# Seven block products summed in PSUM for six pairs of chunks, and the first batch's scores with tokens on partitions

## Chip, core and metric

One core of a Trainium2 chip runs the whole kernel in one launch. The metric is the device time of one execution in microseconds; the median of several runs is compared. TensorE is PE in the profile, VectorE DVE, ScalarE ACT, GpSimd POOL; SyncE (SP) issues the DMAs.

## What is computed

Three stages follow each other: an attention over 32 learned memory slots, a two-layer product with a leaky activation, and a bilinear product. Four batches of 8 heads, 576 tokens and 64 dimensions give 2304 tokens of 512 values.

```python
a = exp(phi - max(phi, axis=2)); a = a / (sum(a, axis=2) + 1e-9)      # over the tokens
k_m = einsum('bhsm,bhsd->bhmd', a, k); v_m = einsum('bhsm,bhsd->bhmd', a, v)
scores = q @ k_m.T / sqrt(64)                                          # 32 per token and head
attn = softmax(scores); x = attn @ v_m                                 # then to (2304, 512)
h = x @ w_in; g = maximum(0.01 * h, h); x = g @ w_out                  # 512 -> 2048 -> 512
out = ((x @ w_a) * (x @ w_b)) @ w_out2                                 # 512 -> 1536 -> 512
```

All values are float32, except that the five weights arrive as 64-bit words, whose two halves the kernel joins into float32 itself.

## The kernel before

Values lie with features on partitions and tokens along the free dimension, so that every product's output is the next one's moving operand. A float32 operand is split in a high and a low part of type fp32r (a copy, on ACT or DVE, and a subtraction), and a product runs as three passes (PASSES, L771): high by high, high by low, low by high. Only in the first chunk for the first batch (FULL, `whole`, L722) are the products plain float32 matmuls, which need no split.

**Attention.** `kv_part` (L547) loads phi, keys and values of a batch and a half of its heads (g), takes the exponential, turns it on PE (ta, tz), sums keys and values against it (km, L603), normalises (kvn), turns again (kvt) and puts the results in kd (for the scores) and vm (for the values), with two copies each. `sc_both` (L653) does the scores of a piece of tokens (320 or 256 columns): the matmuls of L667 leave memory slots on partitions and tokens along the free dimension, so DVE turns them in blocks of 32 (L688), takes the maximum over 32 (L697), subtracts it (L698), ACT takes the exponential (L699), DVE sums (L702 to L704), multiplies (L707) and turns back into the tile at (L711). `vw_unit` (L732) multiplies vm by w_in, so that the attention's last product and the first layer are one: h is made from at and vw (`h_unit`, L803 for the first batch, L821 for the rest).

**The first layer pair.** Four chunks of 512 of the 2048 hidden values (c = 0 to 3), eight pieces of tokens each, in the order 0, 1, 2, ...; for each piece four h units and then four y units (`y_unit`, L867 and L871), one for each 128 rows of the 512 outputs (e). Each y unit reads all four tiles wout of its chunk. `weight` (L451) loads a tile of 128 rows (512 KB) and joins the words with two ACT and four DVE operations.

**The bilinear product.** The 2304 tokens are cut into two sets s of four blocks (2 x 2 of 512 tokens each) and a remainder of 256. For each set there are 12 chunks of 128 of the 1536 hidden values. `ab_unit` (L1076) makes both factors with seven products of a Strassen-Winograd scheme in place of eight, each six matmuls of 512 columns (L1092), in three PSUM banks X, Y and Z; the bank X is a running sum out of which ACT copies after three of its four products (L1103). The remainder goes the plain way (`left_unit`). The last product, by w_out2, works on pairs of chunks. In the plain way `o_unit` (L1168) does eight units of six matmuls (L1186) and DVE adds each into an accumulator in SBUF (L1199). For the pairs of the first eight chunks of the second set (`by_seven`, SEVEN = 8) it goes by seven block products: `w2_sums` makes four sums of the weights, `p_sums` four differences of the tokens and seven splits, and `o_part` (L1286) does product i for half x with three matmuls (L1301) in a PSUM bank of its own, which is added into one of seven accumulators osum (L1326); after the last pair, sums between the accumulators (L1318) make the four outputs. The stores are issued as soon as an output is complete (L1205); the last outputs are those of block l = 1, stored in two parts of 320 and 192 columns.

**The order of the work.** Nothing is ordered by hand. Each operation is given a cost, its tiles and its inputs, and a planner (`Program`, L108) simulates the five engines and lays out each engine's instructions before the kernel is built: the operation with the earliest due time that is ready goes next, on the engine among its candidates that would finish first. Due times come from a target order of the main products (`pos`), costs and handoffs, and are shifted by constants (SLACK for a load's or an operation's kind; START, LEAD, LAT, SPARE for the whole). Tiles get places (slots) as they come free, so a different order also moves loads. PE begins with WARM turns of the identity (L426), and `idle` puts groups of four turns (L434) in the start, each behind an operation whose result it reads: four groups on the tiles of w_in, four on the exponentials en, four on vwf.

Of the kernel before, what the change touches and what calls it, by code (L numbers as in the profile page):

```python
# [19 lines left out]
P = 128  # L20
# [5 lines left out]
EPS = 1e-9  # L26
# [28 lines left out]
TURN = 0.15  # L55
FILL = 4
WARM = 38
SEVEN = 8
LEAD = 37
SLACK = {'phi0': 72.94, ('kv0', 0): -15.48, ('kv0', 1): -17.72, 'kvr0': -10.62, ('q0', 0): 4.66, ('q0', 1): 32.32, ('win0', 0): 0.75, ('win0', 1): 103.86, ('wout0', 0): 20.54, ('wout0', 1): -39.84, 'win': -23.08, 'wout': 22.71, 'wa': -4.25, 'wb': -26.57, 'wout2': -2.14, ('sc', 0, 0): 57.16, ('sc', 0, 1): -2.31, ('sc', 1, 0): 13.24, ('sc', 1, 1): 6.37, ('sc', 2, 0): 23.27, ('sc', 2, 1): 24.61, ('vw', 0, 0): 85.06, ('vw', 0, 1): -56.75, ('vw', 0, 2): 18.69, ('vw', 1, 0): 5.23, ('vw', 1, 1): 100.39, ('vw', 1, 2): 9.67}  # L60
START = 15.05
BIAS = 0.52
POOL_BIAS = 9.26
LAT, LAT_SAME, LAT_DMA = 0.503, 0.134, 3.8
OVER = {'DMA': 0.0, 'PE': 0.0, 'ACT': 0.1, 'DVE': 0.019, 'POOL': 0.0}
BLOCKED = 2.31
DMA_RATE = 355000.0
SPARE = {'DMA': 1.27, 'PE': 1.0, 'ACT': 1.03, 'DVE': 1.03, 'POOL': 0.96}
# [39 lines left out]
class Program:  # L108
# [13 lines left out]
    def op(self, eng, cost, fn, r=(), w=(), tiles=(), pos=None, ahead=60.0, keep=0, slack=0.0, soon=False):  # L122
# [6 lines left out]
        o.slack, o.soon = slack, soon  # L129
# [206 lines left out]
def tile_mem_attention__leaky_mlp__bilinear_mlp(  # L336
# [93 lines left out]
    def idle(tile, get, token):  # L430
# [14 lines left out]
        "wout": lambda c, k: w_out[c * FC + k * P:c * FC + (k + 1) * P, :],  # L445
# [5 lines left out]
    def weight(kind, c, k, after=()):  # L451
# [73 lines left out]
    def phi_stats(b, gs, phi, st):  # L525
# [6 lines left out]
            r=e, w=nmx, tiles=[phi],  # L532
# [14 lines left out]
    def kv_part(b, g):  # L547
# [20 lines left out]
        if g == 0:  # L568
            tile_of(rest, "slot", [2, 512], parts=64)
            op("DMA", c_dma(64 * 4096), lambda T: nc.sync.dma_start(T[rest], kv_rest[b]), w=[rest], tiles=[rest], keep=6 if b else 0, slack=0 if b else SLACK["kvr0"])  # L570

# [20 lines left out]
        if b < 2:  # L592
            idle(en, lambda t: t[:, 0, :], (en, 0))
# [4 lines left out]
        def k_m(T):  # L598
            for t in range(5):
                n = P if t < 4 else 64  # L600
                src = T[kvt[t // 2]][:, t % 2, :] if t < 4 else T[rest][:, g, :]
                for h in range(4):
                    nc.tensor.matmul(  # L603
                        T[km][h * M:(h + 1) * M, :], T[en][0:n, t, h * M:(h + 1) * M], src[:, h * P:(h + 1) * P],
                        start=(t == 0), stop=(t == 4),
                    )

        op("PE", 1.5, k_m, r=[(en, 0), (en, 1), *kvt, rest], w=[km], tiles=[en, *kvt, rest, km])
# [21 lines left out]
        def ev_k(T, e):  # L630
# [526 lines left out]
    def by_seven(s, c):  # L1157
        return s == 1 and c < SEVEN

# [286 lines left out]
```

## Time and profile before

| | us |
|---|---|
| median of 3 runs | 787.47 (786.38 to 788.04) |
| the profiled execution's own time | 786.36 |
| its span, first to last instruction | 784.6 |

The profile is of one execution. The span is shorter than that execution's time by what lies around it. Rows below have times in us from the span's start, unless they say ns. In a timeline row the first number is the start, the second the time that the row's instructions take, and in brackets stands how long the engine was idle before and what released it. PEld are weight loads, which run beside the matmuls. The time of one matmul includes its passage through the array, which overlaps the next one's.

### The profile page before, as it was taken

What the parts mean: (1) busy time and instruction counts of PE and PEld (TensorE: products, weight loads), DVE (VectorE), ACT (ScalarE), POOL (GpSimd) and SP (SyncE); (2) the same over time, 40 slices, a digit from 0 to 9 for tenths busy, and PEclk for the clock granted to TensorE, in tenths of its full rate; (3) what the DMA queues carried; (4) which work ended last, traced back from release to release, by engine and by line L of the source; (5) the groups of instructions that cost most, each with busy time, mean ns of one, the idle gap of its engine ahead of it and who ended that gap; (6) DMA issues with size and microseconds to landing.
All of it is one profiled execution on the core that took longest, in us unless ns stands there. A gap on an engine that the chain in (4) does not pass through costs nothing.

```text
span 784.6 us, 12658 instructions
## 1 busy us (share of the span) xinstructions
PE 773.4 (99%) x4822; PEld 663.4 (85%) x4822; DVE 607.2 (77%) x1149; ACT 379.1 (48%) x817; POOL 0.7 (0%) x6
## 2 busy tenths in 40 slices
PE   7899999999999999999999999999999999999997
PEld 6567898989898988998888888888888888888886
DVE  5888988868888865686745899998995667898865
ACT  5767777747465635453445454445332254223210
POOL 0000000000000000000000000000000000000000
PEclk9999999999999999999999999999999999999999
DMA  9993331573247300035867547475488586978503
GB/s 321 384 323 140 99 90 61 192 264 103 82 174 266 124 1 1 1 115 206 293 247 267 185 160 273 161 239 190 164 322 346 178 275 209 354 250 280 179 19 108
DMA packets 56557, 149.99 MB, mean 191 GB/s; under 512 B 7216, under 2 KB 22576, under 8 KB 56496
## 3 DMA queue, kind: packets, MB, share of 16 engines
q1 hardware_dynamic: 56496, 149.18, 54.5%
q8 instruction: 38, 0.62, 0.3%
q14 instruction: 23, 0.19, 0.1%
HBM read 103.55 MB, written 45.61 MB: 190 GB/s over the span
## 4 chain that ended last, share of the span: by engine, by line
PE 95%; DMA 2%; DVE 1%; SPq 0%; ACT 0%; issue 0%
PE y L871 24%; PE abx L1092 17%; PE o L1186 13%; PE h L821 13%; PE abz L1092 8%; PE os L1301 5%; PE aby L1092 4%; PE b L1146 2%; PE a L1146 2%; PE y L867 2%; PE vw L750 2%; DMA kv<-in_kv_dram 1%; DMA phi<-in_phiT_dram 1%; PE h L803 1%; PE km L603 1%; PE sc L667 0%
## 5 line engine op out<-in xcount | busy, mean ns | idle before, releaser
L871 PE MATMUL y<-g,wout 128*128 128x320 f32 (+2 forms) x1104 | 197.2, 333 | 0.0
L871 PEld LDWEIGHTS y<-g,wout 128*128 128x128 f32 x1104 | 175.6, 188 | 16.7 <-issue 2.1
L1092 PE MATMUL abx<-yb_T,wo 128*128 128x512 f32 x432 | 109.7, 389 | 0.0
L1103 ACT COPY t<-abx 128x512 f32<-128x512 f32 x72 | 42.3, 587 | 122.7 <-PE abx L1092 117.6
L1092 PEld LDWEIGHTS abx<-yb_T,wo 128*128 128x128 f32 x432 | 80.6, 188 | 16.4
L1186 PE MATMUL o<-p,wout 128*128 128x512 f32 x384 | 93.6, 389 | 0.0
L1186 PEld LDWEIGHTS o<-p,wout 128*128 128x128 f32 x384 | 71.9, 188 | 15.2 <-DVE osum L1199 0.4
L774 ACT ACTIVATE g<-h 128x256 fp32r<-128x256 f32 (+1 forms) x120 | 49.7, 414 | 52.9 <-PE h L821 50.8
L821 PE MATMUL h<-ahi,vwh 128*128 128x256 f32 (+1 forms) x240 | 72.7, 303 | 0.0
L821 PE MATMUL h<-ahi,vwl 128*128 128x256 f32 (+1 forms) x240 | 71.0, 296 | 0.0
L821 PE MATMUL h<-alo,vwh 128*128 128x256 f32 (+1 forms) x240 | 71.0, 296 | 0.0
L890 DVE TENSOR_TENSOR acc<-y,acc 128x320 f32<-128x320 f32 (+1 forms) x72 | 40.1, 557 | 36.6 <-PE y L871 35.7
L837 DVE TENSOR_TENSOR g<-t,g 128x256 fp32r<-128x256 f32 (+1 forms) x120 | 53.7, 453 | 15.4 <-ACT t L774 14.4
L821 PEld LDWEIGHTS h<-ahi,vwh 128*128 128x128 f32 x240 | 45.4, 189 | 10.2 <-issue 3.6
L774 ACT ACTIVATE t<-h 128x256 f32<-128x256 f32 (+1 forms) x120 | 49.5, 413 | 0.0
L821 PEld LDWEIGHTS h<-alo,vwh 128*128 128x128 f32 x240 | 45.4, 189 | 0.2
L821 PEld LDWEIGHTS h<-ahi,vwl 128*128 128x128 f32 x240 | 45.5, 190 | 0.0
L1100 DVE TENSOR_TENSOR t<-abz,t 128x512 f32<-128x512 f32 x48 | 33.0, 688 | 13.2 <-PE abz L1092 7.6
L1199 DVE TENSOR_TENSOR oacc<-o,oacc 128x512 f32<-128x512 f32 x40 | 27.6, 690 | 16.7 <-PE o L1186 16.2
L1092 PE MATMUL abx<-yb_B,wo 128*128 128x512 f32 x144 | 36.9, 391 | 0.0
L1092 PE MATMUL aby<-yb_B,wo 128*128 128x512 f32 x144 | 36.7, 390 | 0.0
L407 ACT CAST p<-t 128x512 fp32r<-128x512 f32 x32 | 19.9, 621 | 34.7 <-DVE t L1124 22.7
(289 smaller groups left out, 1276.1 us busy)
## 6 DMA issues: line engine op xcount, KB each, us to landing
k_wo<-wo SPq DMA_DIRECT2D x32, 512.0 KB, 4.4
wo<-k_wo SPq DMA_DIRECT2D x32, 512.0 KB, 4.9
raw_wout<-in_w_out_dram SPq DMA_DIRECT2D x24, 512.0 KB, 5.5
raw_win<-in_w_in_dram SPq DMA_DIRECT2D x16, 512.0 KB, 5.2
kv<-in_kv_dram SPq DMA_DIRECT2D x16, 512.0 KB, 10.4
k_yb_T<-yb_T SPq DMA_DIRECT2D x8, 512.0 KB, 5.9
raw_wa<-in_w_a_dram SPq DMA_DIRECT2D x8, 512.0 KB, 4.5
raw_wb<-in_w_b_dram SPq DMA_DIRECT2D x8, 512.0 KB, 5.4
```

The lines of the kernel that those rows point to most:

```text
L774: nc.scalar.activation(dst, src, AF.Prelu, alpha=0.01)
L821: nc.tensor.matmul(T[o], T[w[u]][:, k, fs], T[a[v]][:, k, cols], start=(k == 0 and i == 0), stop=(k == 1 and i == 2))
L837: lambda T, e: engines[e].tensor_tensor(T[g][:, i, 1, to], T[t], T[g][:, i, 0, to].bitcast(F32), op=ALU.subtract),
L871: nc.tensor.matmul(T[o], w[:, u, es], T[g][:, j, v, at:at + m], start=(f == 0 and p == 0), stop=(f == 3 and p == 2))
L890: "DVE", c_dve(m), lambda T: nc.vector.tensor_tensor(T[acc][:, i, :], T[o], T[acc][:, i, :], op=ALU.add),
L1092: nc.tensor.matmul(T[o], T[w][:, which, u, k * P:(k + 1) * P], T[ys[v]][:, k, :], start=first and k == 0 and x == 0, stop=k == 1 and x == ...
L1100: op("DVE", 0.69, lambda T: nc.vector.tensor_tensor(T[to], T[o], T[x], op=ALU.add), r=[o, x], w=[to], tiles=[o, x, to])
L1103: op("ACT", 0.59, lambda T: nc.scalar.copy(T[t], T[X]), r=[X], w=[t], tiles=[X, t])
L1146: nc.tensor.matmul(T[o], T[w][:, k // 2, u, k % 2 * P:(k % 2 + 1) * P], T[ys[v]][:, k, :], start=(k == 0 and x == 0), stop=(k == 3 and x = ...
L1186: nc.tensor.matmul(T[o], T[w][:, u, es], T[g][:, at, v, :], start=(x == 0 and k == 0), stop=(x == 1 and k == 2))
L1199: "DVE", c_dve(size), lambda T: nc.vector.tensor_tensor(T[acc][:, i, :], T[o], T[acc][:, i, :], op=ALU.add),
L1301: nc.tensor.matmul(T[o], lhs(T, u), T[g][:, v, :], start=k == 0, stop=k == 2)
```

## The change

- The planner's constants are others, and NUDGE shifts the due times of some 230 single operations, by their number. WARM is 41, LEAD 75.
- SEVENS: by seven go the pairs of chunks (10, 11) of the first set and (0, 1) to (8, 9) of the second. The last pair of the second set stays plain.
- `o_part` keeps products 1, 6, 7 and 4 in one bank as a running sum, out of which ACT copies after 1, 6 and 7; product 2 has a bank of its own, products 5 and 3 share one. Each output takes its sum from these: output 2 is product 2 plus the copy after 1, output 7 product 5 plus the copy after 7, output 3 products 5 and 3 plus the copy after 6, output 4 the whole sum. For a first pair (q = 0) one DVE addition makes an output; for a later one there is an addition out of PSUM and, except for output 4, one in SBUF. The accumulators are four, not seven.
- In the last chunk's last unit the 512 columns are done in two units of 320 and 192, each with its addition and its store.
- `sc_tokens` takes the place of `sc_both` for batch 0. The tokens (128 at a time, the last block overlapping the one before it if the piece has 320) are the stationary operand, so scores come with tokens on partitions; maximum and difference are taken straight from PSUM, and the result is turned back on PE and copied into at.
- The first chunk goes through its pieces in the order 1, 0, 2, ...; the first chunk of w_out is loaded in tiles of 256 columns by 256 rows, so that a y unit reads two tiles.
- For batch 0, km takes the rest tile first, then the four blocks in two parts, each waiting for its own tile; the copies into kd and vm are four operations in place of two.
- Groups of filler turns are left out: those on the first two tiles of w_in, on en of batch 1, and all on vwf.

```diff
+SCT = 0.115
-WARM = 38
-SEVEN = 8
-LEAD = 37
+NUDGE = {
...
+FIRST = (1, 0, *range(2, NPIECE))
+KM_FIRST = (((4,), (0, 1), (2, 3)), ((4,), (0, 1), (2, 3)))
+WARM = 41
+SEVENS = ((10, 11), tuple(range(10)))
+LEAD = 75
...
-        o.slack, o.soon = slack, soon
+        o.slack, o.soon = slack + NUDGE.get(o.seq, 0.0), soon
...
-        "wout": lambda c, k: w_out[c * FC + k * P:c * FC + (k + 1) * P, :],
+        "wout": lambda c, k: w_out[c * FC + k * P:c * FC + (k + 1) * P, :] if c else
+        w_out[2 * (k % 2) * P:2 * (k % 2 + 1) * P, k // 2 * 256:(k // 2 + 1) * 256].rearrange("(j p) f -> p j f", p=P),
...
-        if kind == "win" and c == 0:
+        if kind == "win" and c == 0 and k > 1:
             idle(cv, lambda t: t[:, 0, 0:P].bitcast(F32), a)
...
-        if kind == "wout2" and by_seven(1, c):
+        if kind == "wout2" and (by_seven(0, c) or by_seven(1, c)):
...
-        if b < 2:
+        if b == 0:
             idle(en, lambda t: t[:, 0, :], (en, 0))
...
+    def sc_tokens(b, x):
...
+        def s_sc(T, t, c0):
+            for g in range(2):
+                for j in range(2):
+                    for i in range(2):
+                        k, half = 2 * g + j, slice(i * 64, i * 64 + 64)
+                        nc.tensor.matmul(
+                            T[scs[i]][:, t, k * M:(k + 1) * M], T[qs[g]][half, j, c0:c0 + P], kd[b % 2][half, k, :], start=True, stop=True,
+                        )
...
+        for i, o in enumerate(scs):
+            here = mx[:, i * NM:(i + 1) * NM]
+            op(
+                "DVE", c_dve(w), lambda T, o=o, here=here: nc.vector.tensor_reduce(here, rows(T[o]), axis=AX.X, op=ALU.max),
+                r=[(o, t) for t in range(nb)], w=[("mxt", x, i)], tiles=[o],
+            )
+            op(
+                "DVE", c_dve(w), lambda T, i=i, o=o, here=here: nc.vector.tensor_tensor(rows(T[sm][:, i]), rows(T[o]), wide(here, NM), op=ALU.subtract),
...
+            def turn(T, i=i, o=o):
+                for t, c0 in enumerate(at0):
+                    nc.tensor.transpose(T[o][:, c0:c0 + P], T[sm][:, i, t, :], ident)
+
+            op("PE", 0.13 * nb, turn, r=[toks[i]], w=[o], tiles=[sm, o])
+            op(copy_by(n, True), 0, lambda T, e, i=i, o=o: copy(e, T[at][:, i, :], T[o]), r=[o], w=[(at, i)], tiles=[o, at], slack=SLACK["tok", x])
...
-                if b == 0:
-                    idle(fk, lambda t, i=i: t[:, i, x * n:x * n + P], (fk, i, x))
...
-        ws = [("wout", c, f) for f in range(4)]
+        ws = [("wout", c, f) for f in range(4)] if c else [("wout", 0, 2 * (e // 2) + i) for i in range(2)]
...
-    O_PARTS = ((1, "A11", "B11"), (6, "S2", "T2"), (7, "S3", "T3"), (5, "S1", "T1"), (2, "A12", "B21"), (4, "A22", "T4"), (3, "S4", "B22"))
+    O_PARTS = ((1, "A11", "B11"), (2, "A12", "B21"), (6, "S2", "T2"), (7, "S3", "T3"), (4, "A22", "T4"), (5, "S1", "T1"), (3, "S4", "B22"))
...
+        bank = {2: "y", 5: "z", 3: "z"}.get(i, "x")
+        o, g = ("os", s, q, x, bank), ("pb", s, q, right)
+        if i in (1, 2, 5):
+            tile_of(o, "y", [NB2])
...
-                nc.tensor.matmul(T[o], lhs(T, u), T[g][:, v, :], start=k == 0, stop=k == 2)
+                nc.tensor.matmul(T[o], lhs(T, u), T[g][:, v, :], start=i in (1, 2, 5) and k == 0, stop=k == 2, skip_group_check=True)
...
+        if i in (1, 6, 7):
...
+            op("ACT", 0.59, lambda T: nc.scalar.copy(T[k][:, x, :], T[o]), r=[o], w=[(k, x)], tiles=[o, k])
+            return
+        d, m = {2: (2, 1), 4: (4, None), 5: (7, 7), 3: (3, 6)}[i]
...
+        op("DVE", 0.69, lambda T: nc.vector.tensor_tensor(into(T), T[o], into(T), op=ALU.add), r=[o], w=[tok(d)], tiles=[o, acc(d)])
+        if m:
+            op(
+                two(NB2), 0, lambda T, e: engines[e].tensor_tensor(into(T), into(T), T[k][:, x, :], op=ALU.add),
...
-        for n in range(NPIECE):
+        for n in (range(NPIECE) if c else FIRST):
...
-            for i in range({NC2 - 2: 4, NC2 - 1: 1}.get(c, 7) if s else 6):
+            for i in range({NC2 - 2: 6, NC2 - 1: 6}.get(c, 8) if s else 6):
...
-                    queue.extend(lambda pos, c=c, x=x, i=i: o_part(c // 2, x, i, pos) for i in range(7) for x in range(2))
+                    queue.extend(lambda pos, s=s, c=c, x=x, i=i: o_part(s, c // 2, x, i, pos) for x in range(2) for i in range(7))
+                    if not s:
+                        queue.extend(lambda pos, s=s, c=c, e=e: o_unit(s, c - 1, 2, e, pos) for e in range(4))
...
+                        last = s == 1 and c == NC2 - 1 and l == 1 and e == 3
+                        for cols in [p[:2] for p in places_of(s, l)] if last else [None]:
+                            queue.append(lambda pos, s=s, c=c, l=l, e=e, cols=cols: o_unit(s, c - 1, l, e, pos, cols))
```

## Rows read from the trace of the kernel before

**Rows 1.** The page's busy time of PE and DVE (share of the span, instructions).

```profile
PE 773.4 (99%) x4822; PEld 663.4 (85%) x4822; DVE 607.2 (77%) x1149; ACT 379.1 (48%) x817; POOL 0.7 (0%) x6
```

**Rows 2.** Busy time by stage: PE, PEld, DVE, ACT, POOL (instructions), clock, DMA share, GB/s.

```profile
8.00:20.50 12.50, 8.97 (x128) 6.11 (x128) 7.82 (x20) 6.98 (x18) 0.00 (x0) 1.00 1.05 361
...
33.00:43.00 10.00, 9.20 (x51) 6.43 (x52) 9.22 (x20) 9.81 (x27) 0.00 (x0) 1.00 1.04 400
43.00:366.00 323.00, 323.00 (x2391) 285.50 (x2392) 257.00 (x519) 191.85 (x467) 0.00 (x0) 1.00 0.36 125
...
640.00:760.00 120.00, 120.00 (x531) 99.37 (x530) 96.40 (x159) 37.57 (x65) 0.00 (x0) 1.00 0.68 231
760.00:784.60 24.60, 20.65 (x90) 16.44 (x88) 12.16 (x18) 1.83 (x3) 0.00 (x0) 1.00 0.24 86
```

**Rows 3.** One unit in the chain; then groups of lines, 640 to 748 us and whole span.

```profile
421.20 1.36 PE o L1186 x6
...
L1186 PE MATMUL o<-p,wout 128*128 128x512 f32 x384 | 93.6, 389 | 0.0
...
L1326 DVE TENSOR_TENSOR osum<-os,osum 128x512 f32<-128x512 f32 x42 | 28.6, 687 | 3.5 <-PE os L1301 3.0
...
L1318 DVE TENSOR_TENSOR osum<-osum,osum 128x512 f32<-128x512 f32 x14 | 8.9, 683 | 0.0
...
L1103 ACT COPY t<-abx 128x512 f32<-128x512 f32 x72 | 42.3, 587 | 122.7 <-PE abx L1092 117.6
```

**Rows 4.** The end: chain, last issues, landing of a store, and two prices from elsewhere.

```profile
766.76 13.90 PE o L1186 x60
...
780.69 0.69 DVE osum L1199
...
778.69 3.52 SPq L1205 DMA_DIRECT2D out_dram<-osum  x6
...
out_dram<-osum SPq DMA_DIRECT2D x4, 160.0 KB, 1.8
...
L1199 DVE TENSOR_TENSOR oaccl<-o,oaccl 128x256 f32<-128x256 f32 x20 | 8.3, 421 | 4.7 <-PE o L1186 4.5
...
381.20 1.43 PE a L1146 x12
```

**Rows 5.** Timeline of the start, from the head copies to the first y matmuls.

```profile
20.56 0.46 DVE L409 COPY kd<-kvt 64x64 f32<-64x64 f32 x2 [2.17 <-ACT vm L407]
...
22.26 0.86 PEld L434 LDWEIGHTS warm<-ident,vwf 128*128 128x128 f32 x8 [0.41 <-issue]
...
23.29 0.77 PE L667 MATMUL sc<-q,kd 64*32 64x320 f32 x16
...
29.09 0.63 ACT L699 ACTIVATE sm<-sm 128x512 f32<-128x512 f32 x1 [0.32 <-DVE sm L698]
...
31.08 0.68 DVE L702 TENSOR_REDUCE sr<-sm 128x16 f32<-128x512 f32 x1
...
31.15 0.69 ACT L470 ACTIVATE cv_wout<-raw_wout 128x512 f32<-128x512 f32 x1 [1.43 <-DMA raw_wout<-in_w_out_dram]
...
32.88 0.65 DVE L707 TENSOR_TENSOR sm<-sm,sr 128x512 f32<-128x512 f32 x1
33.01 3.50 PE L803 MATMUL h<-at,vwf 128*128 128x320 f32 x12 [0.33 <-DVE at L711]
...
39.46 2.86 PE L803 MATMUL h<-at,vwf 128*128 128x256 f32 x12 [0.78 <-ACT gf L774]
...
40.33 1.28 DVE L488 CUSTOM_DVE_ANT_0 cv_wout<-cv_wout 128x1024 uint16<-128x1024 uint16 x2
...
42.84 3.50 PE L867 MATMUL y<-gf,cv_wout 128*128 128x320 f32 x12
```

**Rows 6.** Warm turns by stretch of one microsecond: PE, PEld, clock, DMA share, GB/s.

```profile
4.00:5.00 1.00, 1.00 (x6) 1.00 (x5) 1.00 1.04 404
...
6.00:7.00 1.00, 1.00 (x11) 1.00 (x10) 1.00 1.02 373
```

More of the change, by code (lines that the diff above doesn't have):

```diff
@@ L62 @@
+START = 30.38
 BIAS = 0.52
[L63 to L66, printed above, removed]
+POOL_BIAS = 19.78
+LAT, LAT_SAME, LAT_DMA = 0.424, 0.288, 6.42
+OVER = {'DMA': 0.0, 'PE': 0.0, 'ACT': 0.1, 'DVE': 0.057, 'POOL': 0.0}
+BLOCKED = 5.85
 DMA_RATE = 355000.0
-SPARE = {'DMA': 1.27, 'PE': 1.0, 'ACT': 1.03, 'DVE': 1.03, 'POOL': 0.96}
+SPARE = {'DMA': 1.17, 'PE': 1.0, 'ACT': 1.03, 'DVE': 1.03, 'POOL': 1.4}
 def c_dve(n):
@@ L596, in kv_part, with k_m @@
         tile_of(km, "x", [P])
-        def k_m(T):
-            for t in range(5):
+        def k_m(T, ts, first, last):
+            for t in ts:
                 n = P if t < 4 else 64
-                src = T[kvt[t // 2]][:, t % 2, :] if t < 4 else T[rest][:, g, :]
+                src = T[kvt[t // 2]][:, t % 2, :] if t < 4 else T[rest][:, g, 0:512]
                 for h in range(4):
@@ L670, in s_sc @@
                         )
[L672 removed]
+        op("PE", 4 * n / 2.4e3 + TURN, s_sc, r=[*qs, *(("kd", b % 2, g, i) for g in range(2) for i in range(2))], w=scs, tiles=[*qs, *scs])
         NM = n // 32
@@ L1314, in o_part @@
         tok = lambda i: (acc(i), x)
-        def plus(d, a):
-            op(
-                two(NB2), 0, lambda T, e: engines[e].tensor_tensor(part(T, d), part(T, d), part(T, a), op=ALU.add),
-                r=[tok(a)], w=[tok(d)], tiles=[acc(a), acc(d)], ahead=1e12, soon=True,
-            )
-        if q == 0:
-            op({"ACT": c_act(NB2), "DVE": c_dve(NB2)}, 0, lambda T, e: copy(e, part(T, i), T[o]), r=[o], w=[tok(i)], tiles=[o, acc(i)])
-            return
-        last = q == SEVEN // 2 - 1
@@ L1326, in o_part @@
-        op("DVE", 0.69, lambda T: nc.vector.tensor_tensor(part(T, i), T[o], part(T, i), op=ALU.add), r=[o], w=[tok(i)], tiles=[o, acc(i)])
-        if not last:
-            return
-        for d in {1: (2, 6), 6: (7, 3), 7: (4,), 5: (3, 7)}.get(i, ()):
-            plus(d, i)
+        kept_of = lambda j: ("ok", s, q, j)
+        if i in (1, 6, 7):
+            k = kept_of(i)
+            if x == 0:
+                tile_of(k, "slot", [2, NB2])
+            op("ACT", 0.59, lambda T: nc.scalar.copy(T[k][:, x, :], T[o]), r=[o], w=[(k, x)], tiles=[o, k])
+            return
@@ new lines, in o_part, with into @@
+        d, m = {2: (2, 1), 4: (4, None), 5: (7, 7), 3: (3, 6)}[i]
+        def into(T):
+            return T[acc(d)][:, x, :]
+        if q == 0 and m is None:
+            op({"ACT": c_act(NB2), "DVE": c_dve(NB2)}, 0, lambda T, e: copy(e, into(T), T[o]), r=[o], w=[tok(d)], tiles=[o, acc(d)])
+            return
+        k = kept_of(m) if m else None
+        if q == 0:
+            op("DVE", 0.69, lambda T: nc.vector.tensor_tensor(into(T), T[o], T[k][:, x, :], op=ALU.add), r=[o, (k, x)], w=[tok(d)], tiles=[o, k, acc(d)])
+            return
```

172 lines of the change are left out of this document (122 added, 50 removed).

## Prediction

> **What bounds the kernel now.** I read the page's busy times first: PE works 773.4 of 784.6 us, DVE 607.2 [rows 1]. An average over stages, so next the busy time stage by stage [rows 2]: from 43 us to the end of the matmuls PE is busy in every microsecond (323.00 of 323, 120.00 of 120), while in 760 to 784.6 us it has 20.65 of 24.60. So three things set the time: when PE begins its unbroken run, how much matmul work the run holds, and what follows its last matmul. DVE, at 96.4 of 120 us in the last stage but one, decides nothing there as long as PE doesn't wait for it.
>
> The middle is a sum of matmuls at a fixed pace: a unit of six 128x512 matmuls takes 1.36 us in the chain [rows 3], 0.227 us each (the 389 ns that the lines give for one overlap the next).
>
> The end: the chain has 60 matmuls of L1186 to 780.66 us, a DVE addition to 781.38, and then the last stores, to 784.6 [rows 4].
>
> The start is where time is lost. The timeline [rows 5] has the head copies kd done at 21.02 us, the scores' matmuls at 23.29, the first h matmul only at 33.01, a hole of 0.78 us before 39.46, and the first y at 42.84. Between scores and h lies one chain on DVE (turn, maximum, difference, sum, product, turn back, two pieces interleaved). Meanwhile DMA runs at full share [rows 2].
>
> **The change, part by part.**
>
> *Seven products.* A pair of chunks costs 8 units of 6 matmuls (L1186), 48; by seven products 14 parts of 3 (L1301), 42. Two more pairs take that way (one in the first set of columns, one in the second): 2 x 6 x 0.227 = **2.7 us less on PE**, all inside its unbroken run, so all on the path.
>
> What it adds beside the path: per new pair one more 0.5 MB load and its two stores, four weight differences, four token differences, seven splits in place of four. These go to ACT and DVE. The additions don't get fewer: before, 42 of L1326 for three pairs [rows 3], 14 a pair; after, 8 out of PSUM and 6 in SBUF, 14 again, plus six ACT copies of 0.59 us. Only the 14 closing sums of L1318 (8.9 us [rows 3]) go. The first set's new parts run where the second set begins, beside work of the ordinary kind. I cost all this at nothing: PE's cover is the 9.5 us of ab products in each chunk. If DVE falls behind, a PSUM bank comes free late and PE pays that delay in full.
>
> *The running sum in PSUM.* Products 1, 6, 7 and 4 now add up in one bank, with an ACT copy after 1, 6 and 7 that must end before the next product may write; 3 likewise waits for DVE's reading of 5. Four such waits for each half, 48 in six pairs. An exposed one costs the copy plus the matmul's own tail: 0.59 + 0.39 - 0.23 + about 0.1 for the handoffs, 0.85 us. The ab products do the same already: 72 copies of abx by L1103 [rows 3], and PE shows no hole there. Bounds: 0 (all covered by ab products between) to 48 x 0.85 = 41 us; I take 0, since the ab rows are the same pattern on the same engines.
>
> *The end.* The last unit is cut in 320 and 192 columns. Its last addition shrinks from 0.69 us to about 0.36 (a 256-wide one takes 0.42 [rows 4]), and one store instead of two is issued after it: six issues fill 3.52 us, 0.59 each; the landing behind it, 1.8 us, stays. Against it, six matmuls of 320 and six of 192 replace six of 512: at the pace of 256 columns (12 in 1.43 us) the short ones cost about 0.11 each, so +0.2. Together **-0.7 us**; bounds 0 (both stores wait on landing anyway) and -1.0.
>
> *The first batch's scores.* Moves and prices:
> - Batch 0 begins with the 256-column piece. Its scores become two blocks of tokens, eight products each; a product is two instructions (sc has 16 for eight), so 16 loads of 128 columns a block. Eight such loads took 0.86 us [rows 5], 0.108 each: a block costs 1.72 us in series, 0.86 if the two halves of 64 rows load side by side; the sc group that it replaces took 0.77. Two blocks: 1.7 to 3.4 us; I take 2.4, nearer the low end, as the sc row (16 instructions in 0.77 us) shows the halves overlapping.
> - By the Trainium skill ("TensorE: Matmul & The Clock Gate", Part 3: Packing small matmuls), a weight load passes matmuls in flight only where its row group differs, which the halves do; by it the sum would take the low end, 0.7 us earlier. No row shows it for 128-column loads of 64 rows.
> - DVE loses the turns in and out. What stays for 256 columns: two maxima and two differences straight from PSUM at about 0.42 each, 1.7; exp 0.63 on ACT; sum with its two small steps 1.17 (31.08 to 32.25); product 0.65; then two turns a half on PE and a copy, 0.6 + 0.4; five handoffs of about 0.15. Sum 5.9 us, against 8.95 from the end of sc (24.06) to h (33.01).
> - Sixteen of the fillers on PE (two groups of eight on vwf, 0.86 us of loads each [rows 5]) stood ahead of or between the scores; they go, with those of two weights and of batch 1. The scores can start at 21.2 instead of 23.29.
> - The head copies split in two operations of the same two copies, the products on the keys take the rest tile first: nothing, or a few tenths earlier.
> So the first h is due at 21.2 + 2.4 + 5.9 = 29.5 us. Early end 28.8 (blocks overlap); late end 23.3 + 3.4 + 5.9 + 2.0 = 34.6, if the scores still queue behind vw and DVE mixes in the other piece's work. I take 29.5, **3.5 us earlier**.
>
> Is the gain kept? Next late is wout. Its first tile could be read at 31.15 and the last conversion ended at 41.61 [rows 5]. The change loads the first w_out in column halves, so the first two y units of a piece need two tiles, half of that DVE work, some 36 to 37 us. Between first h and first y lay 9.8 us; from 29.5 that gives 39.3, later than 37, so it is kept.
>
> *Order.* The loads, due times and nudges are all new. The queue on SP is in order, each load waits behind those ahead of it, so a load placed wrongly can delay everything; moved the right way it gains. What the first h needs (phi, keys and values, half the queries, w_in) is about 5.6 MB, at 361 GB/s [rows 2] 15.5 us from the first issues at 1 us; with some 7 us for conversions, vw and its copies h can't begin much before 24 to 26 (an estimate). I count 3 us more as the most that order alone brings.
>
> **The sum.** -2.7 - 0.7 - 3.5 = -6.9 us. The span of 784.6 becomes 777.7, the profiled execution's 786.36 becomes 779.5. The median of the runs, 787.47, lies 1.1 above that execution, so against it I forecast **780.5 us**.
>
> **The rivals.**
>
> *1. The start doesn't move* (wout or the queries land no earlier and PE fills with the same holes, or the token blocks eat what the turns gave). For: DMA is full until 43 us and raw_wout's wait for its DMA was 1.43 us. Against: the scores stood 2.3 us ready and unserved. Only products and end remain: 787.5 - 3.4 = 784.1.
>
> *2. Loads in better order*, 3 us more: 777.5, and 775.5 with holes gone too.
>
> *3. Slower: PE waits for the copies of the running sum.* Where a part follows its predecessor in the bank with nothing between, 0.85 us is lost. Eight exposed waits of 48 eat the 6.9 us; from ten it is slower by over 0.2%. A quarter exposed, 12, gives 790.7. For it: DVE is 80% busy in that stage, two banks serve all parts. Against it: the ab rows, and that ab products of 1.36 us can lie between, longer than 0.85.
>
> *4. PE loses its clock at the start*, because fillers go and turns come. The granted clock is 1.00 in every row, the higher level; the pace of the warm turns, though, is 6 a microsecond at 4 to 5 us and 11 at 6 to 7 [rows 6], so a stretch at half pace exists. If the stretch from 21 to 33 us ran at it, the token blocks and first h would cost some 4 us more: 784.5.
> By the Trainium skill (same page, Part 4: PE-mode transpose) turns don't count as work that keeps PE's clock up. By that rule this is the likelier course; the trace disagrees so far, since the pace rose during turns alone.
>
> **How the numbers follow.** My forecast has a chance of 0.50 (778 to 783), rival 1 0.18, rival 2 0.17, rival 3 0.07, rival 4 0.05; 0.03 is for a load that delays the start by more than the gain. The range: rival 2's low side at 775.5 holds most of it, and 785.0 takes in rivals 1 and 4; what lies out is rival 3, the late load and the edges, under 2 in 10. A difference under 0.2% (1.6 us) can't be told from none. Faster by more than that means under 785.9: all of the forecast and rival 2, nearly all of 1 and 4, 0.86. Slower, over 789.0, is rival 3 and part of the late load: 0.08. The rest, 0.06, is no change.
>
> **What would show it.** Right: L1301's successor with 252 matmuls instead of 168, L1186's 512-column ones down by 96; the first h near 29.5 us and no hole over 0.5 us before the first y; one store issued after the last addition. Wrong: idle time of PE before os, released by an ACT copy; a first h at 33 us or later with its wait on a load; turns at 0.15 us apiece after 21 us; PE not fully busy after 43 us.

## The result, and the profile after

The changed kernel takes 795.88 us (median of 4 runs, 792.27 to 798.59) where the kernel before takes 787.21 on the same chip: ratio 1.0107, 95% interval 1.0059 to 1.0156. It is **slower**, by 1.1%; 780.5 us was forecast. The profiled execution took 792.27 us with a span of 790.5, 5.9 more than before. One run below, of a kernel with fewer fillers, took 1969.34 us and is left out of that kernel's ratio.

The page of the changed kernel: busy times, and the granted clock in 40 slices.

```profile
PE 778.2 (98%) x4845; PEld 668.2 (85%) x4845; DVE 623.9 (79%) x1190; ACT 395.5 (50%) x843; POOL 0.7 (0%) x6
...
PEclk9699999999999999999999999999999999999999
```

PE is busy 4.8 us longer than before [rows 1], although the last product needs 12 matmuls of 512 columns fewer. The second slice says why to look at the start. Its stages, in the columns of [rows 2]:

```profile
8.00:20.50 12.50, 9.24 (x138) 6.28 (x136) 6.17 (x17) 7.42 (x20) 0.00 (x0) 0.95 1.04 372
20.50:33.00 12.50, 12.04 (x104) 10.57 (x102) 9.30 (x20) 5.46 (x15) 0.00 (x0) 0.50 1.03 353
33.00:43.00 10.00, 9.57 (x120) 6.65 (x126) 5.22 (x13) 7.07 (x20) 0.00 (x0) 1.00 1.04 402
43.00:60.00 17.00, 15.62 (x141) 10.21 (x126) 16.80 (x35) 12.36 (x29) 0.00 (x0) 1.00 0.89 286
...
640.00:760.00 120.00, 119.04 (x524) 97.89 (x523) 97.69 (x161) 51.23 (x89) 0.00 (x0) 1.00 0.60 200
760.00:790.50 30.50, 26.87 (x122) 21.90 (x120) 18.60 (x29) 5.37 (x9) 0.00 (x0) 1.00 0.20 69
```

From 20.5 to 33 us the granted clock is 0.50, the lower of the two levels (1.2 GHz), while PE is 96% busy. PE's own window shows where it falls, 0.2 us ahead of the first token product (19.55) and behind two idle stretches of 0.64 and 1.19 us:

```profile
19.30:19.55 0.25, 0.25 (x11) 0.56 1.19 416
```

From 43 to 60 us PE is busy 15.62 of 17 us, where before it was never idle, and DVE 16.80. And PE idles 0.96 us between 640 and 760. The timeline of the start:

```profile
18.65 0.97 PE L854 MATMUL vw<-cv_win,vm 64*32 64x256 f32 x16 [1.19 <-ACT vm L411]
19.55 7.04 PE L685 MATMUL sct<-kd,q 64*128 64x32 f32 x64
...
27.55 1.92 PE L685 MATMUL sct<-kd,q 64*128 64x32 f32 x16
...
29.50 1.02 DVE L715 TENSOR_REDUCE mx_t<-sct 128x12 f32<-128x384 f32 x2 [1.93 <-PE sct L685]
...
31.36 0.68 DVE L734 TENSOR_TENSOR sm<-sm,sr_t 128x512 f32<-128x512 f32 x1
...
33.67 1.13 PE L905 MATMUL h<-at,vwf 128*128 128x256 f32 x4 [0.42 <-ACT at L411]
...
40.02 0.67 ACT L475 ACTIVATE cv_wout<-raw_wout 128x512 f32<-128x512 f32 x1
...
50.31 2.97 PE L971 MATMUL y<-gf,cv_wout 128*128 128x256 f32 x13
```

A token block (16 instructions) takes 1.74 us here. The product of the first piece (31.36) stands in DVE's in-order queue behind the maxima of the second (29.50), which waited 1.93 us for the fifth block; its own inputs were ready at 27.57. So the first h comes at 33.67, not at 29.5. And the first conversion of w_out begins at 40.02, where before it began at 31.15 [rows 5], so the first y comes at 50.31, not at 42.84. The first load of w_out is issued at 22.91 here and at 20.39 before, 2.5 us later; the rest of the delay is ahead of the conversion in ACT's queue, for ACT isn't idle waiting for that load.

The changed kernel around 646 us, in the timeline:

```profile
639.52 2.92 SPq L1456 DMA_DIRECT2D out_dram<-oacc  x5
...
642.49 5.86 SPq L1314 DMA_DIRECT2D out_dram<-oaccl  x7
...
645.76 1.52 PE L1196 MATMUL abz<-yb_T,wo 128*128 128x512 f32 x6
646.68 0.62 ACT L411 CAST w<-w2s 128x512 fp32r<-128x512 f32 x1 [2.81 <-DMA out_dram<-oacc]
647.37 0.59 ACT L411 COPY osum<-os_x 128x512 f32<-128x512 f32 x1
...
648.01 0.97 PE L1412 MATMUL os_x<-pb_B,wout 128*128 128x512 f32 x3 [0.72 <-ACT osum L411]
```

PE waits for the copy of a running sum. That copy takes only 0.59 us; it is late because the cast ahead of it in ACT's queue stood 2.81 us, released by the landing of a store (out_dram<-oacc), which had read the slot that the cast writes to.

The groups of the last product, behind 372 us:

```profile
L1293 PE MATMUL o<-p,wout 128*128 128x512 f32 x282 | 70.5, 390 | 0.5 <-DVE osum L1306 0.5
...
L1432 ACT COPY ok<-os_x 128x512 f32<-128x512 f32 x36 | 21.2, 588 | 21.3 <-PE os_x L1412 19.9
...
L1412 PE MATMUL os_x<-pb_B,wout 128*128 128x512 f32 x36 | 10.2, 392 | 0.7 <-ACT osum L411 0.7
...
L1412 PE MATMUL os_z<-pb_B,w 128*128 128x512 f32 x36 | 10.2, 392 | 0.2 <-DVE osum L1444 0.2
```

The units of 512 columns went from 384 [rows 3] to 282, 12 shorter ones beside them; of the running sums' matmuls only two groups have idle time ahead.

The end, in the timeline:

```profile
777.26 10.15 PE L1293 MATMUL o<-p,wout 128*128 128x512 f32 x48 [0.55 <-DVE osum L1306]
...
787.46 0.36 DVE L1306 TENSOR_TENSOR osum<-o,osum 128x192 f32<-128x192 f32 x1 [0.33 <-PE o L1293]
```

From the end of the matmuls (787.41) to the end of the span are 3.09 us; before, 780.66 [rows 4] to 784.6, they were 3.94.

**Where the 5.9 us are.** The first matmul of the remainder's factor a (L1250, before L1146) starts at 387.92 us, before at 381.04: the start lost 6.9. From it to the end of the last matmul are 399.5 us in the changed kernel and 399.6 before, so of the 2.7 us of the last product 0.1 is left; PE's holes behind 372 us (0.72, 0.23 and 0.55 us, each with a slower restart behind it) take some 2 of them. The end gives 0.85, and 6.9 - 0.1 - 0.85 is 5.9. As plans differ in what stands ahead of that first matmul, I use another ruler below: the matmuls left at 420 us at 0.227, 0.147 or 0.116 us (512, 320, fewer columns). With the new last product and the start of before (a run below) 356.2 us are left there; in the changed kernel 363.1, 6.8 behind.

### The profile page after: what moved, and what is told of

Same layout as the page of the kernel before. It is cut to its first block, busy times and chain, and to the rows that moved or that the text cites. A ratio compares the mean times of both kernels' runs of the same rounds, so it can differ in the third digit from the quotient of the medians.

```text
span 790.5 us, 12815 instructions
## 1 busy us (share of the span) xinstructions
PE 778.2 (98%) x4845; PEld 668.2 (85%) x4845; DVE 623.9 (79%) x1190; ACT 395.5 (50%) x843; POOL 0.7 (0%) x6
## 4 chain that ended last, share of the span: by engine, by line
PE 94%; DMA 2%; DVE 2%; ACT 1%; issue 0%; SPq 0%; DVEq 0%; ACTq 0%
PE y L975 24%; PE abx L1196 16%; PE h L923 12%; PE o L1293 10%; PE abz L1196 8%; PE aby L1196 4%; PE os_x L1412 4%; PE vw L854 2%; PE b L1250 2%; PE a L1250 2%; PE y L971 2%; PE os_z L1412 2%; PE km L608 1%; PE sct L685 1%; PE os_y L1412 1%; DMA wout<-k_wout_-1_3130 1%
## 5 line engine op out<-in xcount | busy, mean ns | idle before, releaser
L975 PE MATMUL y<-g,wout 128*128 128x320 f32 (+2 forms) x1104 | 200.2, 334 | 0.0
L1293 PE MATMUL o<-p,wout 128*128 128x512 f32 (+2 forms) x294 | 72.2, 386 | 0.5 <-DVE osum L1306 0.5
L1293 PEld LDWEIGHTS o<-p,wout 128*128 128x128 f32 x294 | 54.6, 188 | 12.2 <-DVE osum L1306 1.1
L1196 PE MATMUL abz<-yb_B,wo 128*128 128x512 f32 x144 | 36.7, 390 | 0.0
L1196 PE MATMUL abz<-yb_T,wo 128*128 128x512 f32 x144 | 36.6, 389 | 0.0
```

The source lines that it names most:

```text
L975: nc.tensor.matmul(T[o], w[:, u, here], T[g][:, j, v, at:at + m], start=(f == 0 and p == 0), stop=(f == 3 and p == 2))
L1196: nc.tensor.matmul(T[o], T[w][:, which, u, k * P:(k + 1) * P], T[ys[v]][:, k, :], start=first and k == 0 and x == 0, stop=k == 1 and x == ...
L1293: nc.tensor.matmul(T[o], T[w][:, u, es], T[g][:, at, v, here], start=(x == 0 and k == 0), stop=(x == 1 and k == 2))
```

## Experiments

Each run gives its median and, as a ratio with its 95% interval, its comparison with runs of the kernel before on the same chip, whose medians were 787.06 to 787.51 us.

### The start: four parts one by one

**Holes filled.** Turns where PE idled ahead of the fall (10, 5 and 10, three like this):

```diff
+            for _ in range(10 if (c, b, x) == (0, 0, 1) else 0):
+                nc.tensor.transpose(T[os[0]][:, 0:P], ident, ident)
```

> The changed kernel with 25 more turns of the identity put into three holes of PE (10 before the first ta, 5 before the second kvt, 10 before the first vw), plan otherwise the same. Theory A (the idle stretch of PE between 16 and 18.7 us costs it its clock, and half pace from 19 to 33 us delays the whole start): granted clock 1.00 everywhere after 8 us, a token block takes about 0.87 us instead of 1.74, first h near 28.5 us, time 785 to 788. Theory B (the token products, 32 columns each, are themselves too little work to hold the clock): the clock still reads 0.50 somewhere between 20 and 33 us and the time stays within 2 us of 792 to 798.

792.41 us, 1.0052 (1.0030 to 1.0075). PE, then the granted clock:

```profile
16.00:20.00 4.00, 3.78 (x51) 1.00 1.08 370
20.00:24.00 4.00, 4.00 (x60) 0.75 1.04 411
24.00:32.00 8.00, 7.24 (x53) 0.50 1.02 333
```

The first four token blocks, in the timeline:

```profile
19.63 4.89 PE L689 MATMUL sct<-kd,q 64*128 64x32 f32 x64
```

The clock now falls at 22.04 us, 2.4 us into the token products, with PE busy 4.00 of 4 us. So the holes ahead are not the only cause: in the changed kernel the clock falls behind them before the token products begin, and with the holes filled it falls among the token products. Until the fall a block takes 0.89 us (its pairs of instructions start 0.11 us apart), where the changed kernel has 1.74. The first h comes at 31.60, 2.1 us earlier, but the first y at 50.1 all the same.

**The fillers alone**, taken out of the kernel before:

```diff
-        if kind == "win" and c == 0:
+        if kind == "win" and c == 0 and k > 1:
...
-        if b < 2:
+        if b == 0:
...
-                if b == 0:
-                    idle(fk, lambda t, i=i: t[:, i, x * n:x * n + P], (fk, i, x))
```

> The kernel before, with only the filler turns left out that the change leaves out (two groups on w_in, two on the second batch's exponentials, four on vwf). If those fillers alone held the clock: granted clock under 1.00 in the start, 3 to 8 us slower (790 to 795). If the clock is lost only through the new order or the token products: clock 1.00, and time within 1 us of before, or up to 1 us less since the scores no longer queue behind turns.

790.1 us, 1.0030 (1.0015 to 1.0046), mean clock 0.993 to 1.00 from run to run. Dropping them costs some 2.4 us. The profiled run has a clock of 1.00 and shows no stretch at half clock; three of the nine runs compared lie at 0.993 to 0.996, and of the 23 of the kernel before one does (0.996). So without these fillers the clock falls in some runs; where in them it falls was not profiled.

**The old scores** in the changed kernel:

```diff
-        if b == 0:
-            sc_tokens(b, x)
-            return
```

> The changed kernel with the old scores (memory slots on partitions, DVE turns) for the first batch, all else as changed; the planner lays the start out anew. Theory A (holes cost the clock): clock still falls below 1.00 near 19 us unless the new plan has no hole there, time 789 to 795. Theory B (token products cost it): clock 1.00 in the start, time 784 to 787. If neither start nor clock were the cause but the last product: still 792 or more with clock 1.00.

791.76 us, 1.0045 (1.0029 to 1.0060). The clock is at the lower level only at 27 to 31 us (0.57) and 51 to 58 us (0.51), behind idle PE. The first y is as late as 54.64 us, waiting 1.68 us for a conversion of w_out. So w_out's lateness does not come from the token scores.

**The nudges read.** NUDGE's keys are strings, the operation's number that is looked up is an integer: every lookup of the changed kernel gives 0.0, and its order is the one without nudges.

```diff
-        o.slack, o.soon = slack + NUDGE.get(o.seq, 0.0), soon
+        o.slack, o.soon = slack + NUDGE.get(str(o.seq), 0.0), soon
```

> The changed kernel with its table of nudges read: its keys are strings and the lookup is by a number, so the changed kernel's plan is the same as with an empty table. Theory C (the plan that the nudges describe has no idle stretch before the token products, and the result was slow because the nudges are not applied): clock 1.00, first h near 29 us, 778 to 783. Theory A or B without C: the clock falls here too, 788 to 798.

787.15 us, 0.9996 (0.9982 to 1.0011): the loss is gone, 8.7 us between the medians and 4.4 between the profiled spans (790.5 and 786.1). First y at 46.84. The two profiled spans have the same mean clock (0.991), while two of the four runs of the changed kernel have a lower one, so part of the 8.7 may be clock. And the clock falls as before:

```profile
16.00:20.00 4.00, 1.80 (x24) 0.95 1.08 372
20.00:33.00 13.00, 13.00 (x120) 0.50 1.03 374
33.00:40.00 7.00, 7.00 (x101) 0.98 1.04 362
```

So the plan decides between slower and the same, and the clock is a second loss beside it.

### The clock over the token products

With the nudges read, turns in the three holes and 8 ahead of each token block; then plain matmuls in their place (4 a block, each of them two instructions); then these without the nudges (three kernels):

```diff
+            for _ in range(8):
+                nc.tensor.transpose(T[scs[0]][:, t, :], ident, ident)
```

```diff
+            for _ in range(4):
+                nc.tensor.matmul(T[scs[0]][:, t, :], ident, ident, start=True, stop=True)
```

> The changed kernel with nudges read, holes filled with turns of the identity (6, 5, 10) and eight turns more ahead of each of the five token blocks. If turns count as work that holds the clock: granted clock 1.00 from 8 to 36 us, a token block 0.87 us, and although 4 us of turns are added the time is 782 to 786. If turns don't count (or token products pull the clock down anyway): the clock still falls to 0.50 between 18 and 24 us and the time is 787 to 791, more than with nudges alone because of the added turns.

> The same kernel with plain float32 matmuls of the identity in place of the turns, of about the same PE time (3, 3, 5 in the holes, four ahead of each token block). If the clock fell because the engine did too little in and between the token blocks: clock 1.00, 782 to 786. Against the run with turns: if both hold the clock the two agree within 1 us; if only matmuls do, this one is 4 us or more the faster.

> The changed kernel as it is (nudges not read) with plain matmuls in its holes (5, 3, 5) and four ahead of each token block. If the clock is the main loss: clock 1.00, 785 to 788. If the rest of the loss is the plan (the first w_out converted only after 40 us, first y at 50 us, as in the run with filled holes): first y still at 47 us or later and 788 to 791 in spite of a clock of 1.00.

788.21 us (1.0013, 1.0003 to 1.0023), 788.20 (1.0018, 1.0008 to 1.0027) and 796.31 (1.0117, 1.0100 to 1.0135). With turns, windows and two lines of the timeline:

```profile
20.00:24.00 4.00, 4.00 (x50) 1.00 1.03 377
24.00:32.00 8.00, 7.99 (x99) 1.00 1.03 339
```

```profile
20.32 1.08 PE L691 MATMUL sct<-kd,q 64*128 64x32 f32 x16
21.34 1.09 PE L686 MATMUL sct<-ident 128*128 128x128 f32 x8
```

The clock is 1.00 throughout with either filling, and a block takes 1.02 us to the start of the turns behind it. Turns hold it as well as matmuls; the Trainium skill's rule ("TensorE: Matmul & The Clock Gate", Part 4: PE-mode transpose) that transposes don't count as PE work is not borne out here. The holes were filled in all three kernels, so what the filling among the blocks does alone isn't shown. Five blocks and their eight turns each take 10.2 us, where five blocks at half clock take 8.7. Without the nudges a full clock in the start helps nothing: first y at 51.26 and 796.31 us (part of that is lost at 650 us, as shown below).

With fewer turns a block, 3 and 5 (the same edit):

> The changed kernel with its nudges read and turns in the three early holes (6, 5 and 10), with 3 turns ahead of each token block in place of 8. Five blocks with 8 turns took 10.2 us, half of it turns, at full clock. Theory A (light filling is enough to keep the clock): clock 1.00 from 16 to 40 us, the start 3.2 us shorter than with 8 turns if the softmax is ready as early, 788.2 less up to 3.2 is 785.0. Rival (the token blocks are too large a share again): the clock falls to 0.50 somewhere between 20 and 35 us and the time stays between 787 and 789.

> The same with 5 turns ahead of each token block. Theory A: clock 1.00, 788.2 less up to 1.9 is 786.3. Rival as for three turns; if it falls with three and not with five, the share that the light blocks may take lies between.

Three turns: 787.35 us, 1.0002 (0.9988 to 1.0017), mean clock under 1.00 in 10 of 12 runs. Five: **785.71 us, 0.9979** (0.9971 to 0.9988), clock 1.00 in all 11. PE's windows, first with three and then with five:

```profile
24.00:28.00 4.00, 4.00 (x40) 0.56 1.01 300
28.00:32.00 4.00, 4.00 (x28) 0.50 1.03 393
```

```profile
24.00:28.00 4.00, 4.00 (x61) 1.00 1.01 264
28.00:32.00 4.00, 3.79 (x51) 1.00 1.03 399
```

The nudged kernel and five turns a block thus beat the kernel before. The starts side by side (profiled executions; the last column is the ruler above):

| kernel | clock | first y, us | behind at 420 us |
|---|---|---|---|
| before with the new last product | 1.00 | 42.8 | 0 |
| changed | 0.991 | 50.3 | 6.8 |
| changed, holes filled | 0.991 | 50.1 | 7.6 |
| changed, matmuls, no nudges | 0.998 (1.00 until 651 us) | 51.3 | 7.8 |
| nudges read | 0.991 | 46.8 | 3.2 |
| nudges, 8 turns a block | 1.00 | 46.1 | 2.5 |
| nudges, 5 turns a block | 1.00 | 45.6 | 2.0 |

Even the best new start lies 2.0 us behind the old one.

### The last product

**Alone**, the new sums and the split last unit in the kernel before (its own constants; `o_part` and `o_unit` as changed):

```diff
-SEVEN = 8
+SEVENS = ((10, 11), tuple(range(10)))
```

> The kernel before with only the change of the last product (six pairs by seven products, running sums in PSUM, the last unit cut in two); the start and all planner constants as before. By the prediction's sum: 2.7 us less on PE and 0.7 at the end, 783.5 to 784.5, with no idle time of PE between 366 us and its last matmul. If the waits of the running sum eat it (the changed kernel shows holes of 0.7, 0.5 and 0.2 us before os_x, o and os_z): 785.5 to 787.5, the same as before, with such holes in the trace.

787.78 us, 1.0013 (1.0003 to 1.0023): nothing of 3.6 us is left, at a clock of 1.00 and with the old start. Its largest hole, in the timeline:

```profile
642.97 0.59 ACT L407 COPY osum<-os_x 128x512 f32<-128x512 f32 x1 [5.03 <-DMA k_wo<-wo]
643.45 0.59 ACT L1103 COPY t<-abx 128x512 f32<-128x512 f32 x1
...
644.10 1.66 PE L1092 MATMUL abx<-yb_T,wo 128*128 128x512 f32 x6 [2.05 <-ACT t L1103]
```

The same picture as at 646 us of the changed kernel, with another store. The holes over 0.12 us, with the slower restart behind each, sum to some 4.5 us: 2.2 here, 1.0 at 597 to 606, 1.3 at 770 to 774.

**Is it the first set's pair?** Then seven products in the second set alone cure it; beside it the split alone, and the split with five pairs and the old separate sums (queued pieces placed as in the change):

```diff
-SEVENS = ((10, 11), tuple(range(10)))
+SEVENS = ((), tuple(range(10)))
```

```diff
-SEVEN = 8
+SEVEN = 10
```

> The kernel before with the new last product (running sums in PSUM, split last unit), but seven products only for the five pairs of the second set; the first set's pair of chunks 10 and 11 goes by eight as before, so its outputs are finished and stored within the first set. Against the kernel before: 6 matmuls of 0.227 us fewer (-1.4 us) and the end shorter by 0.96. Theory A (the pair of the first set carries its accumulators and their stores into the second set, and ACT's queue stops behind a slot that such a store still reads): the holes of 2.2 us at 641 to 644 and of 1.0 us at 597 to 606 are gone, of the alone-version's holes only the 1.3 us at 770 to 774 may stay, 787.1 - 1.4 - 0.96 + 0 to 1.3 = 784.7 to 786.0. Rival (the holes come from the running sums themselves, because PE needs each bank back before its next product): the holes come back wherever a pair's products stand, some 4 us in all, 787.8 or more.

> The kernel before with only the last unit split in two column ranges with one store each. Theory: the end shortens by the 0.96 us that the changed kernel shows from its last matmul to the end of the span, 786.1. Rival: the split costs PE as much as it saves (6 matmuls more, shorter), 787.1.

> The kernel before with the split last unit and five pairs by seven in place of four, its sums still kept as seven separate accumulators in SBUF. Removes the same 6 matmuls as the kernel with five pairs and running sums. Theory A (running sums are not what makes the holes, the first set's pair is): about the same as that kernel, 784.7 to 786.0. Rival 1 (running sums make holes, separate ones do not): 784.7 here and over 787 there. Rival 2 (the additions of the separate sums, twelve more on DVE, now fall in the last two units and hold PSUM banks there): PE waits for DVE between 755 and 780 and 786 to 787.5 here, under 786 there.

788.36 us (1.0014, 1.0003 to 1.0025), 786.78 (0.9990, 0.9981 to 0.9998) and 790.03 (1.0035, 1.0022 to 1.0047). My theory fell: the hole stands at 633 us instead. The split has a gain of 0.7 us between the medians, and it has a hole too, though no sum was touched. The second set alone, then the split alone:

```profile
633.88 0.62 ACT L407 CAST pb_T<-pT 128x512 fp32r<-128x512 f32 x1 [4.01 <-DMA k_wo<-wo]
...
635.04 2.14 PE L1092 MATMUL abx<-yb_T,wo 128*128 128x512 f32 x6 [1.89 <-ACT t L1103]
```

```profile
707.54 0.62 ACT L407 CAST w<-w2s 128x512 fp32r<-128x512 f32 x1 [4.41 <-DMA out_dram<-oacc]
...
708.69 1.66 PE L1092 MATMUL abx<-yb_T,wo 128*128 128x512 f32 x6 [0.83 <-ACT t L1103]
```

Such a hole can cost twice. Behind the one at 633 us PE's window in the profile of the second set alone shows the clock at its lower level with PE never idle, some 1.7 us more:

```profile
636.00:639.40 3.40, 3.40 (x10) 0.50 0.60 152
```

The same stands behind a hole of 2.25 us in the run with matmuls and without nudges (0.50 from 651.8 to 655.2 us); behind the 2.05 us of the last product alone the clock stays at 1.00.

With the old sums and five pairs PE waits for ACT and DVE at 765 to 773 us (1.6, 1.2 and 0.6 us), the work of the last differences and sums standing too near the end, and 0.7 us at 635, again behind ACT at a store (2.00 us). So with five pairs the running sums are the cheaper form in these plans, and what all of these kernels share is ACT standing at a slot.

**Slots held.** In the planner a slot that a transfer reads is free when the modelled transfer ends, 0.9 us after the issue for 256 KB (0.74 by DMA_RATE, times SPARE's 1.27); in the DMA view of the kernel before, stores of this size take 2.0 us at the very end (out_dram<-osum), but those of the first set's outputs 7.1, the last number of their row (issues, KB each, us to landing):

```profile
out_dram<-oacc SPq DMA_DIRECT2D x4, 256.0 KB, 7.1
```

Held 6 us longer, from 390 us of the plan on:

```diff
-                heappush(ends, (o.end, o.seq))
+                until = o.end + (6.0 if e == "DMA" and o.start > 390.0 else 0.0)
+                heappush(ends, (until, o.seq))
+                heappush(times, until)
```

Four kernels: with the new last product in both sets, in the second set (planned in 5 rounds instead of 6), in the kernel before, and with the split.

> The kernel before with the new last product in both sets, as in the run of it alone, but the planner hands a slot that a transfer reads out again 6 us after the modelled end of the transfer, for transfers planned after 390 us (the order before 600 us on the chip hardly changes). Theory (slots handed out before the store has landed): no wait of ACT for a store over 1 us in front of a hole of PE; the 2.2 us at 641 to 644 go, perhaps the 1.0 us at 597 to 606 too; 787.8 less 2.2 to 3.2 is 784.6 to 785.6. Rival (DVE's load and the banks): holes stay in their size though at other places, 787 to 789. Second rival (the held slots are missed elsewhere, loads of weights come later): PE waits for a load, 788 or more.

> The kernel with five pairs by seven in the second set only, running sums and the split last unit, slots held as above. Theory: the 2.1 us at 632 to 635 and the 1.7 us just behind it go; 788.4 less 2.1 to 3.8 is 784.6 to 786.3. Rival: holes stay, 788 or more.

> The kernel before with slots held as above, as a control. It has no hole of PE over 0.1 us behind 380 us, so by both theories nothing is to be had: 787.0 to 787.6; slower by up to 2 us only if the held slots are missed elsewhere.

> The kernel with only the last unit split, slots held as above. Theory: the hole of 1.0 us at 706 to 709 goes and the whole 0.96 us of the end is gained, 785.9 to 786.5. Rival: 786.8 as without the holding.

786.71 us (0.9989, 0.9980 to 0.9998), 786.76 (0.9994, 0.9986 to 1.0003), 788.16 (1.0009, 1.0000 to 1.0018) and 786.89 (0.9999, 0.9990 to 1.0008). All of PE's waits behind 40 us, with both sets:

```profile
PE h L805 <- ACT gf L776: 0.9, 1, 0.9
PE o L1191 <- DVE osum L1344: 0.5, 1, 0.5
PE o L1191 <- DVE osum L1204: 0.3, 1, 0.3
```

Every wait of PE for an ACT copy that stood behind a store is gone, in all three kernels that had one, and the new last product gains 1.1 us between the medians (787.78 to 786.71, on two chips; 1.0013 to 0.9989 as ratios). That is less than the 2.2 to 3.2 I wrote down: the 1.0 us at 597 to 606 stayed (now at 598 to 608). These small holes are not the slots': PE's weight loads wait there for ACT copies that ended just before (at 598.60 and 602.98, the second a running sum's) and for a DVE addition (607.50); nothing was tried against them. The second set alone gains less than I wrote down too (786.76), the split gained nothing in time although its hole went, and the control itself lost 0.1%.

**The last sums earlier.** Seven queued pieces in place of six in each of the last two chunks, in the kernel just shown with both sets:

```diff
-            for i in range({NC2 - 2: 6, NC2 - 1: 6}.get(c, 8) if s else 6):
+            for i in range({NC2 - 2: 7, NC2 - 1: 7}.get(c, 8) if s else 6):
```

> The kernel before with the new last product in both sets and slots held 6 us longer, with seven queued pieces instead of six placed into each of the last two chunks, so that all partial products of the last pair by seven stand ahead of the closing output units. Theory (PE waits there because the last two partial sums are read by DVE only behind the closing products of the last chunk): the 1.1 us between 768 and 773 go, 786.7 less 1.1 is 785.6. Rival (DVE is late in any order, since it reads both the last sums and the closing products): the holes move, 786.3 to 787.

**785.43 us, 0.9976** (0.9966 to 0.9986). The two waits of o for osum are gone. DVE's addition that frees the bank of the last os_z, first with six and then with seven:

```profile
770.04 0.69 DVE L1344 TENSOR_TENSOR osum<-os_z,osum 128x512 f32<-128x512 f32 x1
```

```profile
767.98 0.84 PE L1310 MATMUL os_z<-pb_B,w 128*128 128x512 f32 x3
...
769.23 0.68 DVE L1344 TENSOR_TENSOR osum<-os_z,osum 128x512 f32<-128x512 f32 x1
```

With six the last os_z stood at nearly the same place (768.03) and already ahead of the output units. What moved is DVE: its products of the last chunk are done earlier, and the addition comes 0.8 us earlier. In the changed kernel an output unit stood ahead of the last os_z and PE waited at 777.26 for DVE. With slots held and this order the new last product is faster than the kernel before by 1.7 us, with its start untouched. This and the nudged start with five turns were not tried together.

## Why the prediction was wrong

- **The start, -3.5 us: measured +6.8.** Three steps failed. *Order*: I wrote that the nudges are all new and that order could only bring up to 3 us; I took from the diff that they act. They don't, and reading them is worth 4.4 us between the profiled spans and 8.7 between the medians. That the change doesn't do what it says was a rival I left out. *"Is the gain kept? ... it is kept"*: I carried over when w_out could be read (31.15) and only cut the DVE work; its first conversion came at 40.02. *The blocks*: 2.4 us for two. Each takes 0.89 us at full clock, so my low end of 1.7 for the first piece would have been near; but it is 1.74 at half, and the second piece's three blocks and maxima get in between, which stood only in my late end (34.6; measured 33.67).
- **Rival 4 saw the loss of the clock**, with 0.05, and half of its reason. I put it low because the warm turns' pace rises in [rows 6]. Fillers that go do cost clock: in the changed kernel it falls behind idle PE at 19.33 us. "Turns come" is not the reason: what holds it down, and brings it down by itself once the holes are filled, are the token products, and turns among them keep it up. It priced 4 us; what can be had back is less, since the turns that restore the clock cost time too: with five a block the ruler goes from 3.2 to 2.0.
- **Seven products, -2.7 us: the saving is there, and all but 0.1 us is given back.** The counts came as forecast: os has 252 matmuls, and the plain units have 96 fewer than before (384 to 288, of which 6 are split in 12). The step that failed is "I cost all this at nothing: PE's cover is the ab products". The cover holds for the work, not for a queue that stands still: with copies of 0.59 us in ACT's queue behind an instruction that stands 2.8 to 5 us at a slot, 1.36 us of ab products are not enough.
- **Rival 3** named the right wait (PE for an ACT copy) and the wrong price: not 0.85 us at many parts, but 0.7 to 2.1 us at one, and what made that copy late was not the running sum itself.
- **The end, -0.7 us: measured -0.85** in the profile. Right.
- The range (775.5 to 785.0) left out rival 3 (0.07) and the late load (0.03). What came has something of both: w_out is late, by its load and by its place in ACT's queue, and PE waits for copies.

Open is why two of the four runs of the changed kernel show a mean clock of 0.985 (797.81 and 798.59 us) and two 0.991 (792.27 and 793.95). If all else is at the upper level, 0.985 is some 24 us at the lower one (2 x 0.015 x 796, an estimate), against 13.65 in the profiled run; no profile of such a run was taken.

## What to carry to other kernels

A saving on the busiest engine counts only if each in-order queue that feeds it still arrives: look at what stands ahead of the copy, and at the slots that stores still read, before a copy is called covered. A hole on PE can cost its own length and then a stretch at the lower clock. A planner that frees a buffer at a transfer's modelled end should free it when the transfer lands. And before pricing a table of tuned constants, see that the code looks them up.

## What the runs showed of the hardware

- PE at 100% busy with token products (64 rows by 128 columns, 32 moving columns) falls from granted clock 1.00 to 0.50 (holes filled: at 22.04 us, with 4.00 of 4 us busy); in that run and in the changed kernel it stays there for 13.65 us. With five turns among every 16 such instructions, and the holes filled, it stays at 1.00 in 11 of 11 runs, with three it falls in 10 of 12.
- Such a block of 16 takes 0.89 us at the upper level, 56 ns an instruction, with blocks in a row, and 1.02 us between turns. The price of two halves in series was 1.72, side by side 0.86. The Trainium skill ("TensorE: Matmul & The Clock Gate", Part 3: Packing small matmuls) would have them side by side; the trace agrees.
- Stores of 256 KB landed 7.1 us after their issue (first set's outputs) or 2.0 us (the last ones). ACT instructions that a store's landing released had waited 2.0 to 5.0 us, and those waits ahead of PE's holes were gone when the planner held slots 6 us longer.
